# Strided convolution with normalisation, forward and backward: first weights over a second hardware queue, two elementwise stages of the second batch on ScalarE, and a re-planned order

## The chip, the core and the metric

The kernel runs on one core of a Trainium2 chip. The core has TensorE (PE: matmuls, with its weight loads shown as PEld), VectorE (DVE), ScalarE (ACT), GpSimd (POOL) and SyncE (SP). DMAs are issued by SP, ACT and POOL, each into a queue of its own; the packets of all three run on the same 16 DMA engines. Each engine works through its own instructions in the order of the program and waits on semaphores for the others. The metric is the device time of one execution in microseconds. Before the change it was 1239.66 us, the median of three runs from 1238.98 to 1240.63.

## The reference

Everything is bfloat16 at the interface: `x` (2, 16000, 256), `w` (31, 256, 256), `gn_gamma` and `gn_beta` (256).

```
L = (16000 - 31) // 2 + 1 = 7985
h[b,l,:]  = sum_i x[b, 2*l + i, :] @ w[i]            i = 0..30
mu, var   = mean and variance of h over l, per b and channel
hn        = (h - mu) / sqrt(var + 1e-5) * gamma + beta
out_0     = gelu(hn)                                  (tanh form)
out_1..4  = gradients of x, w, gamma, beta for the given grad_out (2, 7985, 256)
```

So there are three large products: the forward convolution, its input gradient and its weight gradient. Between the first and the second lies the elementwise part (normalisation, gelu, its derivative, and sums over l).

## The kernel before

**Stages.** The plan names five. F0 is the forward convolution of batch 0 and F1 that of batch 1; under F1 the gelu part of batch 0 runs on ACT and DVE. G0 is the input gradient of batch 0, with the gelu part of batch 1 under it. G1 is the input gradient of batch 1, with the differences that the weight gradient needs (`d2_piece`) under it. W is the weight gradient. A batch is cut into four chunks `c`; a chunk has three branches `br` (B_, A, C_), and in the gradient two halves `pr`. The products are built from sums and differences of inputs and of weights, three in place of four, and that at three levels, so each branch starts with a product (`f_three_b`, `g_three_b`), lets ACT copy it negated within PSUM (L540, L1060), goes on with `three_ac` products, is combined by DVE in PSUM (`f_seed`, `g_seed`, which record `ve` at L583), and ends in `leaf` products whose result ACT moves out (`f_evac`, `g_evac`: L611 or `keep` at L591). PSUM is a ring of four tiles; a branch takes two.

**The start.** `x_load` (L399) brings the odd rows of the first chunk as three plain loads (two of 512 KB, one of 64 KB). PE turns them by matmuls (`x_first`, L419), DVE and ACT put them into SBUF (L431, L429). `load_w` (L443) brings the weights: 16 loads, slots A and C_, two channel halves `ch`, all on SP's queue behind x. `f_first` (L706) forms weight differences on DVE (`w_sub`, L466) and starts the first leaf products. All later chunks of x come as one transposing DMA on SP's queue (`turn`, L346).

**The gelu part.** `gelu_unit` (L829) works on 1024 columns: a load of h on ACT's queue (the `hd` tensor), four ACT instructions (L836, L838, L842, L844), several DVE ones, a store on POOL's queue, a sum on ACT (L860).

**Between gelu and input gradient.** For each chunk `e_load` (L928) loads dy and h (1 MB each) on SP's queue, and `e_comp` (L932) computes h*s5 + s6 (L938), dy*s4 (L941) and their sum (L943) on 2048 columns twice, then spreads the result into padded tiles (four copies: two of 1536 columns, two of 512). The spread goes by `COPY = ("ACT", "DVE")`: on ACT (L953) for batch 0, on DVE (L955) for batch 1. `dn_turn` (L977) transposes the same result and stores it.

**What sets the order.** No operation is emitted where it is written. `Plan.add` records each with its engine, an assumed duration, what it reads and writes, and for a DMA its transfer time. `Plan.order` gives each a due time from the PE work that needs it (less a `slack`, and less a `lead` that is set by hand for each kind of operation), and plays a list schedule: at each engine the ready operation that is due first goes next. PE may take any of the next `look` operations of its own list. `pads` hold a DMA back behind what it depends on; DMAs share one server that takes them one after another, and eight lanes per queue group. The operations are then emitted in the order of their planned starts, and the engines keep that order. `PACE` spreads the gelu units over the PE work. Planned times are used for nothing else.

Of the kernel before, what the change touches and what calls it, by code (L numbers as in the profile page):

```python
# [13 lines left out]
ALU = mybir.AluOpType  # L14
# [24 lines left out]
class Plan:  # L39
# [3 lines left out]
    def __init__(self, tc):  # L43
        self.tc = tc
        self.ops = []
        self.lastw = {}
        self.readers = {}
        self.pe = 0.0
        self.slack = 120.0
        self.hold = -1  # L50
        self.look = 11
        self.pads = (270.0, 253.5, 0.0)
        self.lead = {
            "F0 f_mm f_leaf": 4.0,
            "F0 f_mm f_outer": -1.5,
            "F0 f_mm f_three_ac": 5.5,
            "F0 f_mm pe_turn": 7.5,
            "F0 f_three_b forward": -7.5,
            "F0 keep f_evac": -4.0,
            "F0 load f_evac": 10.5,  # L60
            "F0 load load_w": -2.5,
            "F0 load put": 2.0,
            "F0 tt f_sums": 7.5,
            "F0 tt third": -5.0,
            "F0 turn w2_part": -1.5,
            "F0 turn x_load": -5.0,
            "F0 ve f_seed": -2.0,
            "F0 w_sub f_first": 7.5,
            "F1 f_evac last": -7.5,
            "F1 f_mm f_leaf": -5.0,  # L70
            "F1 f_mm f_three_ac": 1.5,
            "F1 gelu_unit gelu_batch": -3.0,
            "F1 load gelu_unit": 2.5,
            "F1 tiny fwd_stats": -4.0,
            "F1 tt gelu_unit": 1.0,
            "F1 turn gelu_batch": -6.5,
            "F1 turn x_load": -5.0,
            "F1 ve f_seed": 6.5,
            "F1 zero gelu_batch": 11.0,
            "G0 e_comp conv_stem_kernel": -3.0,  # L80
            "G0 g_mm g_leaf": -11.0,
            "G0 g_mm g_three_ac": 5.0,
            "G0 g_mm g_three_b": -4.0,
            "G0 gelu_unit gelu_batch": -0.5,
            "G0 keep g_evac": -3.5,
            "G0 load dgb_store": 7.0,
            "G0 load dn_turn": -8.0,
            "G0 load e_load": 4.5,
            "G0 load g_evac": -8.0,
            "G0 load gelu_unit": 10.0,  # L90
            "G0 load load_w2": 5.0,
            "G0 tiny elem_finalize": 1.5,
            "G0 tt first": 5.0,
            "G0 tt second": 6.0,
            "G0 tt third": 5.5,
            "G0 turn dgb_store": -3.0,
            "G0 turn dn_turn": 1.0,
            "G0 turn gelu_batch": -8.5,
            "G0 ve g_seed": 3.5,
            "G0 ve_neg g_seed": 8.0,  # L100
            "G1 e_comp conv_stem_kernel": -10.0,
            "G1 g_mm g_outer": 3.5,
            "G1 g_mm g_three_ac": 0.5,
            "G1 g_mm g_three_b": 0.5,
            "G1 g_three_b input_grad": 2.5,
            "G1 keep g_evac": -3.5,
            "G1 load dn_turn": 0.5,
            "G1 load e_load": -4.0,
            "G1 load g_evac": 5.5,
            "G1 spread e_comp": -9.5,  # L110
            "G1 tt first": 10.5,
            "G1 tt second": -4.5,
            "G1 tt third": -5.0,
            "G1 zero e_comp": -5.0,
            "W keep weight_grad": 4.0,
            "W load d_tile": -15.5,
            "W load w_emit": -8.5,
            "W ve w_done": 5.0,
            "W ve weight_grad": 9.0,
            "W w_add weight_grad": 2.5,  # L120
            "W w_emit w_done": 7.5,
            "W w_mm w_pairs": -1.5,
            "W w_mm w_single": -1.0,
        }
        self.overlap = {"DVE": 0.084, "ACT": 0.1}
        self.npe = 0
        self.stage = "F0"
# [23 lines left out]
    def add(self, eng, dur, outs, ins, fn, dma=None, slack=None):  # L151
# [24 lines left out]
        self.ops.append(dict(eng=eng, kind=kind, dur=dur, fn=fn, preds=preds, dma=dma, at=self.pe, hold=-1 if eng == "PE" else self.hold,  # L176
# [3 lines left out]
    def order(self):  # L180
# [7 lines left out]
        for i in range(n - 1, -1, -1):  # L188
            o = ops[i]
            full = o["dur"] + (1.3 * o["dma"] + 6.0 if o["dma"] is not None else 0.15)  # L190
            end = o["at"] if o["eng"] == "PE" else o["at"] + o["slack"]
            for s in succ[i]:
                end = min(end, due[s])
            due[i] = end - full - self.lead.get(o["kind"], 0.0)
        left = [len(o["preds"]) for o in ops]
        ready = [0.0] * n
        wait = {e: [] for e in ("PE", "DVE", "ACT", "POOL", "SP")}
        pes = [i for i, o in enumerate(ops) if o["eng"] == "PE"]
        rank = {i: k for k, i in enumerate(pes)}
        nextpe = 0  # L200
        gone = set()
        lanes = [[0.0] * 8, [0.0] * 8]
        for i in range(n):
            if not left[i]:
                wait[ops[i]["eng"]].append(i)
        free = {e: 0.0 for e in wait}
        server = 0.0
        start = [0.0] * n
        ends = [0.0] * n
        done = 0  # L210
        while done < n:
            best = None
            for e, w in wait.items():
                if e == "PE":
# [3 lines left out]
                if w:  # L218
                    t = max(free[e], min(ready[i] for i in w))
                    if best is None or t < best[0]:  # L220
                        best = (t, e, w)
            t, e, w = best
            i = min((i for i in w if ready[i] <= t + 1e-9), key=lambda i: (due[i], i))
            wait[e].remove(i)
            o = ops[i]
            if o["dma"] is not None:
                lane = lanes[e == "POOL"]
                t = max(t, lane.pop(0))
            start[i] = t
            end = t + o["dur"]  # L230
            free[e] = end - self.overlap.get(e, 0.0)
# [5 lines left out]
            if o["dma"] is not None:  # L237
                server = max(server, end + 1.3) + o["dma"]
                end = server + 0.9
                lane.append(end)  # L240
            ends[i] = end
            done += 1
            slip = free["PE"] - due[pes[nextpe]] - ops[pes[nextpe]]["dur"] if nextpe < len(pes) else 0.0
            for s in succ[i]:
                r = end + 0.034 * (e != "PE") if ops[s]["eng"] == e and o["dma"] is None else end + 0.12
                room = max(0.0, due[s] + slip - r)
                if ops[s]["dma"] is not None:
                    r += min(self.pads[0 if o["dma"] is None else 1], 0.3 * room)
                elif o["dma"] is not None and ops[s]["eng"] != "PE":
                    r += min(self.pads[2], 0.3 * room)  # L250
                ready[s] = max(ready[s], r)
                left[s] -= 1
                if not left[s]:
                    wait[ops[s]["eng"]].append(s)
        self.start, self.ends = start, ends
        return sorted(range(n), key=lambda i: (start[i], i))
# [13 lines left out]
def conv_stem_kernel(  # L270
# [64 lines left out]
    def dcost(nbytes, run):  # L335
        ns = {256: 18, 512: 27, 1024: 46, 2048: 85, 4096: 165}[run]
        return nbytes / run * ns / 16e3 * 1.1
# [1233 lines left out]
```

## Time and profile before

| What | us |
|---|---|
| median of three runs | 1239.66 (1238.98 to 1240.63) |
| the profiled execution | 1234.47 |
| its span, first to last instruction | 1232.3 |
| PE busy in the span | 1195.2 (97%) |
| DVE busy | 1010.3 (82%) |
| ACT busy | 535.8 (43%) |
| POOL busy | 203.7 (17%) |
| mean granted TensorE clock | 0.992 |
| DMA | 263.56 MB, mean 214 GB/s |

The profiled execution is 5.2 us shorter than the median of the runs; its span covers all but 2.2 us of it. PE is busy nearly throughout, so what counts is where PE waits and for whom. The profile gives for each wait its length and the instruction that ended it last; a matmul that runs at a lower granted clock is busy, not waiting, so after a long wait the clock column has to be read as well.

### The profile page before, as it was taken

How to read it: one execution, taken by the hardware profiler on the slowest of the kernel's cores; microseconds unless marked ns; L12 is line 12 of the kernel's file. 1: busy time of each engine (PE TensorE's matmuls, PEld its weight loads, DVE VectorE, ACT ScalarE, POOL GpSimd, SP SyncE). 2: the span in 40 equal slices, each digit the busy share in tenths (PEclk: the TensorE clock that was granted, in tenths of full speed). 3: DMA queues.
4: the chain of work that ended last, by engine and by line, in shares of the span. 5: the costliest groups of instructions: out<-in, count | busy, mean ns of one | idle time of the engine just before them, and what ended most of it. 6: DMA issues, size and time to landing. Idle time of an engine off the chain costs nothing.

```text
span 1232.3 us, 19408 instructions
## 1 busy us (share of the span) xinstructions
PE 1195.2 (97%) x7846; PEld 768.7 (62%) x7846; DVE 1010.3 (82%) x1297; ACT 535.8 (43%) x769; POOL 203.7 (17%) x321
## 2 busy tenths in 40 slices
PE   6999999899999999999999999999999999999998
PEld 4888899577676964444444444444466554566865
DVE  7988798597979859989887889888776986778883
ACT  1243344565768468888783334444322111012200
POOL 1020231011111203211210323333210000011031
PEclk8999999899999999999999999999999999999999
DMA  9642979866695896686636888886899499986562
GB/s 205 108 111 63 191 198 177 168 139 158 127 201 159 258 317 208 231 248 168 213 120 182 254 273 313 245 308 251 300 305 326 145 318 319 320 293 218 179 170 69
DMA packets 283545, 263.56 MB, mean 214 GB/s; under 512 B 186815, under 2 KB 254446, under 8 KB 275184
## 3 DMA queue, kind: packets, MB, share of 16 engines
q1 hardware_dynamic: 255808, 166.38, 52.5%
q0 software_dynamic: 23040, 87.55, 20.1%
q10 hardware_dynamic: 4608, 8.39, 2.3%
q8 instruction: 61, 1.00, 0.3%
q14 instruction: 28, 0.23, 0.1%
HBM read 129.44 MB, written 87.52 MB: 176 GB/s over the span
## 4 chain that ended last, share of the span: by engine, by line
PE 79%; DVE 6%; DMA 6%; issue 4%; ACT 2%; POOL 2%; SPq 0%; POOLq 0%; ACTq 0%; DVEq 0%
PE ps L508 31%; PE ps L1289 27%; PE ps L1033 21%; DMA d2d<-arena 2%; DMA arena<-hd 1%; DVE arena L1196 1%; POOL d2d L341 1%; DVE arena L476 1%; DMA out_dram<-arena 1%; DVE ps L583 1%; DMA arena<-in_x_dram 1%; DVE arena L466 1%; DMA arena<-arena 1%; DMA arena<-in_w_dram 1%; DVE arena L943 0%
## 5 line engine op out<-in xcount | busy, mean ns | idle before, releaser
L1033 PE MATMUL ps<-arena 128*128 128x512 bf16 (+1 forms) x2016 | 435.9, 378 | 11.8 <-DVE ps L583 8.3
L508 PE MATMUL ps<-arena 128*128 128x256 bf16 (+4 forms) x3552 | 426.7, 282 | 12.6 <-DMA arena<-in_x_dram 6.9
L508 PEld LDWEIGHTS <-arena 128*128 128x128 bf16 x3552 | 347.8, 99 | 94.4 <-issue 13.7
L1033 PEld LDWEIGHTS <-arena 128*128 128x128 bf16 x2016 | 198.0, 98 | 249.4 <-issue 20.1
L1289 PE MATMUL ps<-arena 128*128 128x256 bf16 (+1 forms) x2176 | 332.5, 313 | 0.0
L1289 PEld LDWEIGHTS <-arena 128*128 128x128 bf16 x2176 | 212.8, 98 | 112.6
L591 ACT ACTIVATE arena<-ps 128x1024 f32<-128x1024 f32 (+1 forms) x143 | 146.1, 1022 | 277.8 <-PE ps L1033 79.9
L476 DVE TENSOR_TENSOR arena<-arena 128x1087 bf16<-128x1087 bf16 (+3 forms) x194 | 163.7, 889 | 27.5 <-PE ps L508 27.2
L850 DVE TENSOR_TENSOR arena<-arena 128x1024 bf16<-128x1024 bf16 x160 | 109.0, 689 | 14.8 <-ACT arena L842 8.2
L1252 DVE TENSOR_TENSOR arena<-arena 128x4096 bf16<-128x4096 bf16 x42 | 95.8, 2288 | 25.2 <-PE ps L1289 19.6
L583 DVE TENSOR_TENSOR ps<-ps,arena 128x1024 f32<-128x1024 f32 x77 | 94.0, 1229 | 27.0 <-PE ps L1289 13.3
L341 POOL DMA_DIRECT2D out_dram<-arena x75 | 54.1, 741 | 365.7 <-DVE arena L1321 292.0
L992 DVE TENSOR_TENSOR arena<-arena 128x516 bf16<-128x516 bf16 (+3 forms) x176 | 83.5, 513 | 16.4 <-PE ps L1033 10.0
L1196 DVE TENSOR_TENSOR arena<-arena 128x768 bf16<-128x768 bf16 (+3 forms) x112 | 65.5, 642 | 16.7 <-DMA d2d<-arena 15.6
L341 POOL DMA_DIRECT2D d2d<-arena x70 | 51.0, 729 | 112.3 <-DVE arena L1196 110.7
L611 ACT ACTIVATE arena<-ps 128x512 bf16<-128x512 f32 (+1 forms) x64 | 36.8, 578 | 74.5 <-PE ps L508 74.5
L840 DVE SCALAR_TENSOR_TENSOR arena<-arena 128x1024 bf16<-128x1024 bf16 x32 | 39.2, 1224 | 20.1 <-ACT arena L838 19.8
L583 DVE TENSOR_TENSOR ps<-arena,ps 128x1024 f32<-128x1024 f32 x43 | 52.8, 1227 | 3.2 <-PE ps L1033 2.7
L1370 ACT COPY ps<-ps 128x512 f32<-128x512 f32 x28 | 16.0, 571 | 87.6 <-PE ps L1289 87.6
L1060 ACT ACTIVATE ps<-ps 128x512 f32<-128x512 f32 x48 | 27.9, 582 | 58.8 <-PE ps L1033 58.6
L1413 DVE TENSOR_TENSOR arena<-arena 128x2304 bf16<-128x2304 bf16 x36 | 48.0, 1354 | 5.5 <-PE ps L1289 5.5
L341 POOL DMA_DIRECT2D dyd<-arena x32 | 17.6, 550 | 194.2 <-DVE arena L850 189.5
(87 smaller groups left out, 785.8 us busy)
## 6 DMA issues: line engine op xcount, KB each, us to landing
arena<-in_x_dram SPq DMA_DIRECT2D x52, 1024.0 KB, 9.6
arena<-d2d SPq DMA_DIRECT2D x16, 1216.0 KB, 11.9
out_dram<-arena POOLq DMA_DIRECT2D x14, 1024.0 KB, 5.9
d2d<-arena POOLq DMA_DIRECT2D x30, 384.0 KB, 6.3
arena<-dnd SPq DMA_DIRECT2D x10, 960.0 KB, 6.4
vl<-arena POOLq DMA_DIRECT2D x36, 256.0 KB, 4.8
arena<-vl SPq DMA_DIRECT2D x9, 1024.0 KB, 8.6
hd<-arena POOLq DMA_DIRECT2D x8, 1024.0 KB, 6.3
```

The lines of the kernel that those rows point to most:

```text
L341: add(eng, issue or {"POOL": 0.8, "SP": 0.4, "ACT": 0.15}[eng], [out], [in_], lambda: e.dma_start(out=out, in_=in_), dma=dcost(nbytes, run ...
L476: lambda: nc.vector.tensor_tensor(out=o, in0=a, in1=b, op=ALU.add))
L508: yield nc.tensor.matmul(ps[:, dh, cs], lhsT=wt, rhs=mv, start=s0, stop=False, skip_group_check=True)
L583: add("DVE", dve(1024, 1), [out], [a, b], lambda: nc.vector.tensor_tensor(out=out, in0=a, in1=b, op=op))
L591: lambda: nc.scalar.activation(out=out, in_=ps, func=ACT.Copy, scale=scale))
L850: add("DVE", dve(1024), [o], [a, b_], lambda: V.tensor_tensor(out=o, in0=a, in1=b_, op=op))
L992: lambda: nc.vector.tensor_tensor(out=o, in0=a, in1=b, op=ALU.add))
L1033: yield nc.tensor.matmul(ps[:, e, 0:wide], lhsT=lt, rhs=mv, start=s0, stop=False, skip_group_check=True)
L1196: lambda: nc.vector.tensor_tensor(out=out, in0=a, in1=b_, op=ALU.subtract))
L1252: add("DVE", dve(4096), [o], [a, b], lambda: nc.vector.tensor_tensor(out=o, in0=a, in1=b, op=ALU.add))
L1289: yield nc.tensor.matmul(ps[:, s, c0:c1], lhsT=lt, rhs=mv, start=s0, stop=False, skip_group_check=True)
L1413: add("DVE", dve(2304), [DL[i3, b]], [D2[b]], lambda b=b, i3=i3, o_=o_: nc.vector.tensor_tensor(out=DL[i3, b], in0=D2[b][:, o_:o_ + 17:2, ...
```

## The change

Four things change.

- The 64 KB load of x and the four weight loads of slot A, `ch` 0, are issued on ACT's queue; the other loads of x and of the weights stay on SP's. The 64 KB load is recorded first.
- `e_comp` of batch 1 does both affine steps on ACT (activations with scale and bias taken from tiles) in place of DVE, and its spread on ACT too.
- The planner's picture of DMAs is replaced. `listing` lets three queues move packets at the same time: on each queue the oldest transfer is active, and active transfers share the engines by the packet time of their shape (`tp`), with a factor `mixed` where transposes run beside others. SP's queue blocks while more than `room` packets are on their way. The costs of an issue and of packets (`SH`, `PK`) are new.
- The hand-set numbers follow: `slack`, `look`, `pads`, all of `lead`, `PACE`. Every engine's order over the whole kernel is therefore new. The set of operations is the same but for the queue and engine moves above: 7846 matmuls in both.

```diff
-        self.slack = 120.0
+        self.slack = 110.0
-        self.look = 11
-        self.pads = (270.0, 253.5, 0.0)
+        self.look = 13
+        self.pads = (375.5, 347.0, 2.5)
         self.lead = {
-            "F0 f_mm f_leaf": 4.0,
...
+            "F0 f_mm f_leaf": 12.5,
...
         }
+        self.room, self.mixed = 2048.0, 1.4
...
+        def flow(t):
+            nonlocal now
+            if total > 0:
+                for x in air:
+                    if x["act"]:
+                        x["rem"] -= (t - now) * x["tp"] / total
+            now = t
+
+        def inflight():
+            return sum(x["rem"] * 16e3 / ops[x["i"]]["ns"] for x in air if ops[x["i"]]["eng"] == "SP")
...
+            heads = {}
+            for x in air:
+                x["act"] = heads.setdefault(ops[x["i"]]["eng"], x) is x and x["on"]
+            total = sum(x["tp"] for x in air if x["act"])
+            if total > max((x["tp"] for x in air if x["act"]), default=0.0) and any(ops[x["i"]]["ns"] < 20.0 for x in air if x["act"]):
+                total *= self.mixed
...
             if o["dma"] is not None:
-                server = max(server, end + 1.3) + o["dma"]
-                end = server + 0.9
-                lane.append(end)
+                k = e == "POOL"
+                air.append(dict(i=i, on=False, act=False, lane=turn[k], rem=o["dma"], tp=o["tp"], t0=end + 1.3))
+                lanes[k][turn[k]] = 1
+                turn[k] = (turn[k] + 1) % 8
+                if e == "SP" and inflight() > self.room:
+                    blocked, spend = True, end
+                continue
...
-            for g, nm in enumerate((P, P, 16)):
-                load(rows[g][0:nm], src[P * g:P * g + nm].rearrange("m (j o f) -> m j o f", j=4, o=2)[:, :, 1, :], nm * 4096, 1024)
+            for g, nm in ((2, 16), (0, P), (1, P)):
+                load(rows[g][0:nm], src[P * g:P * g + nm].rearrange("m (j o f) -> m j o f", j=4, o=2)[:, :, 1, :], nm * 4096, 1024,
+                     "ACT" if g == 2 else "SP")
...
-                         65536 * nq, 512, issue=0.8)
+                         65536 * nq, 512, "ACT" if sl == A and ch == 0 else "SP")
...
-    COPY = ("ACT", "DVE")
+    COPY = ("ACT", "ACT")
...
+            if b == 0:
+                add("DVE", dve(2048, 4), [hv], [hv, s5, s6], ...
+                add("DVE", dve(2048, 4), [ev], [ev, s4], ...
+            else:
+                add("ACT", act(2048, 0.18), [hv], [hv, s5, s6],
+                    lambda hv=hv, s5=s5, s6=s6: nc.scalar.activation(out=hv, in_=hv, func=ACT.Identity, bias=s6, scale=s5))
+                add("ACT", act(2048, 0.18), [ev], [ev, s4],
+                    lambda ev=ev, s4=s4: nc.scalar.activation(out=ev, in_=ev, func=ACT.Identity, scale=s4))
...
-    PACE = ((5.0, 19.0), (391.0, 67.0))
+    PACE = ((20.0, 16.5), (327.0, 54.0))
```

What the new order does at the places the prediction speaks of, read from the two programs (line numbers of the kernel before):

- Start: the weights of both slots for `ch` 0 are loaded before those for `ch` 1, and the leaf products run in that order (A and C_ with `ch` 0, then with `ch` 1); before, slot A came first with both halves.
- Start of F1: on ACT the first load of h, then the square root of the statistics, then the `keep` (L591) of batch 1's first result stand ahead of the first gelu unit; before, two loads of h came first and that `keep` stood behind five instructions of two gelu units. The second load of h now stands behind that `keep`. The big transposing load of x (chunk 1) stays near the same place on SP's queue.
- Chunk 2 of F1: `f_three_b`'s two halves are separated by a leaf product.
- Start of G0: the first `g_three_b` stands ahead of the last two leaf groups of F1 on PE, and its ACT copy ahead of the last evacuations.
- End of G1: the addition of two x tiles for the weight gradient (`w_add`, L1252) that stood between two of the last `g_seed` instructions on DVE stands behind them.

271 lines of the change are left out of this document (155 added, 116 removed).

## The prediction

> **What bounds the kernel now.** I read the busy shares first, then who ends PE's waits, then the places of those waits in order of time.
>
> ```profile
> PE 1195.2 (97%) x7846; PEld 768.7 (62%) x7846; DVE 1010.3 (82%) x1297; ACT 535.8 (43%) x769; POOL 203.7 (17%) x321
> ...
> PE ps L1033 <- DVE ps L583: 8.3, 9, 2.4
> PE ps L508 <- DMA arena<-in_x_dram: 6.9, 2, 4.6
> PE ps L508 <- ACT arena L591: 6.1, 1, 6.1
> PE ps L508 <- DVE arena L476: 4.0, 1, 4.0
> PE ps L508 <- ACT arena L611: 3.5, 2, 1.9
> PE ps L1033 <- ACT arena L611: 2.1, 1, 2.1
> PE ps L1033 <- ACT ps L1060: 0.8, 1, 0.8
> PE ps L1033 <- ACT arena L591: 0.6, 2, 0.3
> ```
>
> PE works 97% of the span, and no matmul is added or removed, so only PE's waits can move the time: 32.3 us in all, 10.9 of them (x, and L476) in the first 15 us, 21.4 later. A wait also lowers the granted clock: 0.95 over 240 to 300 us, 0.94 over 450 to 480, 0.97 over 850 to 900, which is 60*0.05 + 30*0.06 + 50*0.03 = 6.3 us of missing clock. What the new order can win after the start is thus at most 27.7 us. W has no wait of PE from 895 to 1224 us: nothing to win there.
>
> The largest wait, in order of time:
>
> ```profile
> 216.92 20.43 SPq L346 DMA_TRANSPOSE arena<-in_x_dram  x1
> ...
> 219.53 0.91 ACTq L341 DMA_DIRECT2D arena<-hd  x2
> ...
> 232.73 1.24 ACT L836 ACTIVATE arena<-arena,stats 128x1024 bf16<-128x1024 bf16 x1 [10.14 <-DMA arena<-hd]
> ...
> 240.37 1.01 ACT L591 ACTIVATE arena<-ps 128x1024 f32<-128x1024 f32 x1
> ...
> 241.42 0.37 PE L508 MATMUL ps<-zt 128*128 128x256 bf16 x1 [6.11 <-ACT arena L591]
> ```
>
> Two loads of h (256 KB each) are issued 2.6 us into a 20.43 us transposing load of x; ACT stands still for 10.14 us until they land; the `keep` at L591 is queued behind, and PE waits for it. Other loads of this kind take 4.6 us (median): here the queues collide on the shared engines.
>
> The input gradient of batch 1, and the operations that move:
>
> ```profile
> 680.00:720.00 40.00, 37.92 (x179) 17.31 (x178) 33.16 (x48) 16.04 (x22) 11.82 (x18) 1.00 0.89 276
> 720.00:760.00 40.00, 38.82 (x180) 17.35 (x179) 38.68 (x62) 16.23 (x23) 13.52 (x19) 1.00 0.86 275
> ...
> L938 DVE TENSOR_SCALAR arena<-arena,stats 128x2048 bf16<-128x2048 bf16 x16 | 12.6, 812 | 3.5 <-DMA arena<-hd 3.5
> L941 DVE TENSOR_SCALAR arena<-arena,stats 128x2048 bf16<-128x2048 bf16 x16 | 11.7, 750 | 0.0
> L955 DVE COPY arena<-arena 128x1536 bf16<-128x1536 bf16 x8 | 4.2, 559 | 0.0
> L953 ACT COPY arena<-arena 128x1536 bf16<-128x1536 bf16 x8 | 11.6, 1464 | 2.9 <-issue 2.7
> ```
>
> DVE (third column of busy time) is full here, ACT (fourth) at 40%, and all waits of PE but 0.6 us are ended by DVE's `g_seed` (L583).
>
> **The change part by part.** Gains are negative; the bounds stand behind each.
>
> *Start.* SP issued 16 weight loads one after another, 2.81 to 18.41 us; DVE's first `w_sub` waited for one until 12.66, and the first leaf product began at 15.14. Five DMAs leave SP for ACT. Their issue costs 0.33 us each (hd rows): 1.7 us, plus the table load 1.28, before an ACT whose first copy was needed at 9.86; the fifth waits until the 64 KB load has landed (5.5 us), which still ends before. POOL is not touched. x (512 KB twice, landed 7.2) now shares the engines with 1 MB of weights. 2048 packets of 512 B took 3.6 us, 1024 of 1 KB 3.0; taken in turn, x lands about 1.8 us later, the first weights about 1 us earlier. x is then last: PE's turning (3.92 us from 7.19), two copies, `w_sub` 1.23 and the sum 1.29 start the leaf products near 14.5. Gain 0.6; bounds +2 (all of x's delay passes on) and -2 (the 2.3 us wait for x goes). The busy time by stretches shows DMA at 1.11 of the 16 engines from 10 to 20 us, so the engines, not the issue, limit the end of these loads; therefore a value near nothing. The Trainium skill, "DMA: Bandwidth & Descriptors", section "Rules for kernel authors", says that spreading DMAs over SP, ACT and GpSimd gives no bandwidth and saves issue time alone. The 1.11 agrees; by that rule the term would be 0 and the sum 0.6 higher.
>
> *F1's start.* The 241 us place costs 6.1 of wait and 2.0 of slow clock (18 matmuls in 1.91 + 2.67 us where eight take 1.04 at full clock). The `keep` now stands ahead of the gelu units, so this wait goes. What is late next: the second load of h is still issued into the same transposing load, and ACT's next `f_three_b` copy (L540) stands behind its reader. It landed at 235.6, two readers take 2.4, so the copy is done near 239; PE, running on from 235.1, has 2 us of first products and 6 us of leaf work ahead of it. If the load is 3 us later still, 2.6 us are lost. I take -5.5 (0 to -8.1).
>
> *319 and 390 us.* Waits of 1.92 and 1.60 for evacuations (L611) queued behind gelu instructions; at the first, 4.2 us of them. In the new order a leaf product covers the first; the second I cannot tell: -2.5 (0 to -3.5).
>
> *G0's start.* Waits of 2.12, 0.80 and 0.64 from 450 to 481 and 1.8 of clock. Two leaf groups (28 matmuls of 230 columns each, 2.8 us by the 118 that took 11.87 us from 435.77) now lie between the first `g_three_b` and the product that needs its copy; the evacuations on ACT are covered. -3.5 (0 to -5.4).
>
> *G1, DVE.* Batch 1 takes from DVE 8*0.812 + 8*0.750 + 8*0.559 + 8*0.298 (the 512 copies) = 19.4 us. PE's waits there before the last are 8.3 - 0.64 - 2.40 + 0.6 = 5.9 us. About half goes, since `d2_piece` also waits for its stores (15.6 us of DVE's idle time): -3 (0 to -5.9).
>
> *G1, ACT.* No row has an activation over 2048 columns. From 1024 columns with two tile operands (L838, 1.234) and the slope of L953 ((1.464 - 0.614)/1024 columns) it takes 1.234 + 0.85 = 2.08 us. 16 of these, 8 copies of 1.464 and 8 of 0.614 add 49.9 us. ACT from 620 to 895 goes from 41-44% to about 60%. From 500 to 600 us ACT was busy 85.0 of 100 us with instructions of 0.6 to 1.5 us, and PE did not wait once; so a busy ACT is hidden by PE's leaf work as long as nothing ACT waits for is late. The cost is taken as +2, near that row (0 to +18, below).
>
> *890 us.* The last `g_seed` stood behind `w_add`, which waited for x until 886.4: wait 2.40, clock 1.5. `w_add` moves behind; the weight gradient's first product then needs x, 2.3 + 1.2 us of DVE later, and PE has some 5 us before it. -3 (0 to -3.9).
>
> *New waits.* Every engine's order is new, so there will be waits that the old order did not have. The old one had 27.7 us of such cost; I allow about a fifth, +5 (0 to +27.7).
>
> Sum: -0.6 - 5.5 - 2.5 - 3.5 - 3 + 2 - 3 + 5 = -11.1. From the profiled execution, 1234.5 - 11.1 = 1223.4; the median of the runs lay 5.2 above the profiled one, so 1228.6, rounded to 1229.
>
> **The rivals.**
> *ACT blocks the second batch (slower).* For chunks 1 to 3 `e_comp` on ACT waits for two 1 MB loads, with `keep` and copies queued behind. At 232 us such a wait of 10.14 us gave PE one of 6.11, 0.6 of it. Three times 10.14 would cost 18.3 us instead of +2 and take the 3 us of DVE with it: 1229 + 19 = 1248. It decides from about 7 us per chunk (three times 0.6*7 = 12.6, against 11.1 + 2). For it: DMA at 0.85 in this stretch, these loads take 6.4 and 8.5 us. Against: before, DVE waited for them once, 3.5 us. The Trainium skill, "ScalarE: Activation LUTs", "Rules for kernel authors", advises VectorE for multiply and add, being up to about three times faster in bf16. The rows agree (0.81 against the estimate of 2.08), and the advice speaks for this rival.
> *Contention stays (same).* The h load lands as late and blocks ACT at the next copy, DVE's relief is eaten by stores: 5.5 + 3 less gain, 1237.5, between 1235 and 1242.
> *Hidden better (faster still).* No new waits, all of DVE's share: 1229 - 5 - 3 = 1221.
> *W begins to wait (slower).* DMA is at 0.83 to 0.95 from 900 to 1100 and 9.6 us is the median of an x load; three late pairs of 5 us: 1244.
>
> **How the numbers follow.** Forecast 0.45, ACT blocks 0.2, contention stays 0.15, hidden better 0.12, W waits 0.08. 0.2% of the time, 2.5 us, is about what can be told from no change, so same is 1237.2 to 1242.1. Faster: 0.45*0.95 + 0.12 + 0.15*0.4 + some of the last = 0.64; same 0.11, mostly contention; slower 0.25 from ACT and W. The likeliest case alone lies in 1223 to 1236. The range reaches from 1218 (everything hidden) to 1247 (ACT blocks by nearly its full price) and leaves out about 0.2.
>
> **What will show it.** Right: no wait of PE near 241 us ended by L591's counterpart; the first leaf product near 14.5; the waits on `g_seed` in G1 down by about half; activations of 2048 columns at 2.0 to 2.1 us; W still without waits. Wrong: waits of PE ended by ACT in G1 above 5 us in sum, ACT waiting for hd or dyd there, or new waits in F0, where PE did not wait between 15 and 235 us.

## The result and the profile after

The changed kernel takes 1250.59 us (median of 20 runs, 1239.76 to 1256.90), the kernel before 1237.56 (median of 20; 19 of them from 1230.80 to 1245.38, and one of 4483.74, which the median passes over). The ratio is 1.0105, 95% interval 1.0079 to 1.0130: 13 us slower, where 1229 (1218 to 1247) was predicted. The profiled execution took 1246.25 us, its span 1244.5.

Where PE waits now, longest first (the view of waits: us in total, times, longest):

```profile
PE ps L575 <- DMA arena<-in_x_dram: 9.2, 2, 5.1
PE ps L1106 <- DVE ps L650: 8.5, 11, 2.9
PE ps L1362 <- DMA arena<-d2d: 7.7, 2, 4.0
PE ps L575 <- ACT ps L607: 6.4, 2, 5.7
PE ps L575 <- DVE arena L543: 4.5, 1, 4.5
```

Three of these lines are new or longer: the start waits more for x (9.2 against 6.9), the wait of 6.1 for the `keep` at F1's start has become one of 5.7 for a copy (L607), and W, which had no wait, waits 7.7 for d. Against the waits on `g_seed` (L650) little was won: 8.5 in 11 waits, 8.3 in 9 before.

To see what each stage lost or won, I took from each trace the times at which PE's 1750th, 3598th, 4600th, 5614th and last of its 7846 weight loads start. They cut the span near the ends of F0, F1, G0, G1 and W; the orders differ by a few groups of matmuls at the cuts.

| span of (us) | F0 | F1 | G0 | G1 | W | rest | whole |
|---|---|---|---|---|---|---|---|
| before | 207.0 | 240.4 | 218.7 | 228.7 | 332.4 | 5.1 | 1232.3 |
| after | 210.6 | 242.1 | 215.7 | 227.6 | 343.3 | 5.1 | 1244.5 |
| after less before | +3.6 | +1.7 | -3.0 | -1.1 | +10.9 | 0 | +12.2 |

So in this pair of profiles the loss lies in W above all, and in the start. The place in W, on SP's queue and on PE:

```profile
895.38 8.74 SPq L412 DMA_TRANSPOSE arena<-yd  x1
904.31 4.42 SPq L407 DMA_DIRECT2D arena<-in_x_dram  x2
908.82 22.48 SPq L412 DMA_TRANSPOSE arena<-yd  x1
931.40 1.00 SPq L407 DMA_DIRECT2D arena<-d2d  x2
...
937.47 0.60 PE L1362 MATMUL ps<-arena 128*128 128x256 bf16 x4 [4.00 <-DMA arena<-d2d]
941.81 1.01 PE L1362 MATMUL ps<-arena 128*128 128x256 bf16 x4 [3.74 <-DMA arena<-d2d]
```

and SP's queue in the kernel before:

```profile
888.14 17.57 SPq L346 DMA_TRANSPOSE arena<-yd  x2
905.83 1.28 SPq L341 DMA_DIRECT2D arena<-in_x_dram  x2
907.19 3.43 SPq L341 DMA_DIRECT2D arena<-d2d  x2
```

The second column is the time SP was held. `yd` holds y, the gelu output of batch 1 that is transposed late on its way to out_0; `d2d` holds d, the differences that the weight gradient reads. A transposing load of y (1 MB) that took 8.74 us a moment earlier holds SP for 22.48; the two loads of d stand behind it, are issued at 931.4 and come late. In the kernel before both loads of y came one right after the other, and d was issued at 907.19.

F1's start, the same view on SP, ACT and PE:

```profile
223.51 23.57 SPq L412 DMA_TRANSPOSE arena<-in_x_dram  x1
...
243.15 1.24 ACT L903 ACTIVATE arena<-arena,stats 128x1024 bf16<-128x1024 bf16 x1 [13.60 <-DMA arena<-hd]
...
252.97 0.58 ACT L607 ACTIVATE ps<-ps 128x512 f32<-128x512 f32 x1
...
253.60 9.75 PE L575 MATMUL ps<-arena 128*128 128x256 bf16 x56 [5.70 <-ACT ps L607]
```

The wait at 241 us is gone as the `keep` now runs at 228.5, but its cause is as it was: x's transposing load takes 23.57 us (20.43 before), ACT stands still 13.60 us (10.14) for the first load of h, and the copy at L607, behind two gelu units, is the next that PE misses. The size varies: in five other profiles with this order of F1 (the runs d_first, head_on_sp, late_y_plain, affine_on_dve and no_out_store below) the wait here is 4.6, 9.4, 11.1, 11.9 and 15.9 us.

The start, on PE and DVE, after and then before:

```profile
9.52 3.49 PE L575 MATMUL ps<-arena 128*128 128x128 bf16 x31 [4.10 <-DMA arena<-in_x_dram]
...
18.51 7.69 PE L575 MATMUL ps<-arena 128*128 128x512 bf16 x35 [4.50 <-DVE arena L543]
...
15.50 1.22 DVE L533 TENSOR_TENSOR arena<-arena 128x2048 bf16<-128x2048 bf16 x1 [2.08 <-DMA arena<-in_w_dram]
```

```profile
15.14 11.14 PE L508 MATMUL ps<-arena 128*128 128x512 bf16 x55 [4.03 <-DVE arena L476]
12.66 1.23 DVE L466 TENSOR_TENSOR arena<-arena 128x2048 bf16<-128x2048 bf16 x1 [0.25 <-DMA arena<-in_w_dram]
```

x is complete at 9.5 us (7.2 before), and the weights of the first `w_sub` (L533) at 15.5 (12.7). The leaf products begin at 18.51 instead of 15.14. The DMA view of 9 to 13 us (queue: packets, MB, share of 16 engines), after and then before, shows why the weights are later:

```profile
q10 hardware_dynamic: 1209, 0.60, 57.5%
q1 hardware_dynamic: 1133, 0.56, 54.5%
```

```profile
q1 hardware_dynamic: 2317, 1.15, 116.3%
```

The engines move as much as before, 1.16 MB in 4 us. But the four loads that this `w_sub` needs are ScalarE's (q10), and half of what moves is SP's (q1): weights that nobody needs yet. On one queue the needed ones came first.

The input gradient of batch 1 (busy time by stretches), and what ScalarE took over:

```profile
680.00:720.00 40.00, 38.47 (x176) 17.41 (x178) 33.69 (x49) 25.59 (x28) 13.00 (x20) 1.00 0.95 274
720.00:760.00 40.00, 36.24 (x168) 16.39 (x170) 34.17 (x52) 27.29 (x30) 12.96 (x21) 1.00 0.98 289
...
L1012 ACT ACTIVATE arena<-arena,stats 128x2048 bf16<-128x2048 bf16 x8 | 16.4, 2090 | 0.0
L1014 ACT ACTIVATE arena<-arena,stats 128x2048 bf16<-128x2048 bf16 x8 | 15.6, 2000 | 5.0 <-DMA arena<-dyd 5.0
```

ACT is busy 53 of 80 us here (32 before), and DVE 68 (72 before); PE is a little busier in the first stretch (37.92 before) and less in the second (38.82).

### The profile page after: what moved, and what is told of

Its sections match the earlier page's. It is cut to its first block, busy times and chain, and to the rows that moved or that the text cites. A ratio compares the mean times of both kernels' runs of the same rounds, so it can differ in the third digit from the quotient of the medians.

```text
span 1244.5 us, 19368 instructions
## 1 busy us (share of the span) xinstructions
PE 1191.3 (96%) x7781; PEld 768.8 (62%) x7846; DVE 994.6 (80%) x1265; ACT 579.3 (47%) x801; POOL 200.8 (16%) x321
## 4 chain that ended last, share of the span: by engine, by line
PE 62%; DVE 10%; issue 10%; DMA 9%; ACT 5%; POOL 3%; SPq 0%; POOLq 0%; DVEq 0%; ACTq 0%
PE ps L575 25%; PE ps L1362 24%; PE ps L1106 13%; DMA arena<-hd 3%; DVE arena L917 3%; DMA d2d<-arena 2%; POOL d2d L407 2%; DMA out_dram<-arena 1%; DVE ps L650 1%; DVE arena L1269 1%; DVE arena L907 1%; DMA arena<-in_w_dram 1%; DMA arena<-d2d 1%; ACT arena L678 1%; DVE arena L543 1%
## 5 line engine op out<-in xcount | busy, mean ns | idle before, releaser
L1106 PE MATMUL ps<-arena 128*128 128x512 bf16 (+1 forms) x1974 | 430.2, 376 | 15.5 <-DVE ps L650 8.5
L1106 PEld LDWEIGHTS <-arena 128*128 128x128 bf16 x2016 | 197.0, 98 | 248.2 <-issue 12.7
L1362 PEld LDWEIGHTS <-arena 128*128 128x128 bf16 x2176 | 213.5, 98 | 122.4 <-issue 9.4
L543 DVE TENSOR_TENSOR arena<-arena 128x1088 bf16<-128x1088 bf16 (+3 forms) x194 | 162.9, 887 | 13.4 <-PE ps L575 12.9
L917 DVE TENSOR_TENSOR arena<-arena 128x1024 bf16<-128x1024 bf16 x160 | 108.5, 689 | 23.8 <-ACT arena L909 15.5
L650 DVE TENSOR_TENSOR ps<-ps,arena 128x1024 f32<-128x1024 f32 x77 | 93.6, 1227 | 19.8 <-PE ps L1362 14.4
L1065 DVE TENSOR_TENSOR arena<-arena 128x514 bf16<-128x514 bf16 (+3 forms) x176 | 81.1, 511 | 7.2 <-PE ps L1106 4.4
L650 DVE TENSOR_TENSOR ps<-arena,ps 128x1024 f32<-128x1024 f32 x43 | 52.7, 1226 | 12.0 <-PE ps L1106 8.7
L678 ACT ACTIVATE arena<-ps 128x512 bf16<-128x512 f32 (+1 forms) x64 | 36.9, 580 | 52.3 <-PE ps L575 52.1
L650 DVE TENSOR_TENSOR arena<-arena 128x1024 f32<-128x1024 f32 x32 | 38.4, 1221 | 28.0 <-ACT arena L640 17.2
L1486 DVE TENSOR_TENSOR arena<-arena 128x2304 bf16<-128x2304 bf16 x36 | 48.2, 1353 | 12.7 <-PE ps L1362 12.7
L407 POOL DMA_DIRECT2D vl<-arena x36 | 26.1, 726 | 158.5 <-DMA arena<-in_w_dram 99.8
## 6 DMA issues: line engine op xcount, KB each, us to landing
arena<-d2d SPq DMA_DIRECT2D x16, 1216.0 KB, 10.9
```

The costliest lines, as they stand in the source:

```text
L407: lambda: e.dma_start(out=out, in_=in_), dma=np_ * PK[pk] / 16e3 * 1.03, ns=PK[pk], tp=SH[pk], slack=slack)
L543: lambda: nc.vector.tensor_tensor(out=o, in0=a, in1=b, op=ALU.add))
L650: add("DVE", dve(1024, 1), [out], [a, b], lambda: nc.vector.tensor_tensor(out=out, in0=a, in1=b, op=op))
L917: add("DVE", dve(1024), [o], [a, b_], lambda: V.tensor_tensor(out=o, in0=a, in1=b_, op=op))
L1065: lambda: nc.vector.tensor_tensor(out=o, in0=a, in1=b, op=ALU.add))
L1106: yield nc.tensor.matmul(ps[:, e, 0:wide], lhsT=lt, rhs=mv, start=s0, stop=False, skip_group_check=True)
```

## The experiments

All were compared with the kernel before on the same chip. A line of the table gives the ratio with its interval and the stage spans of the profile, cut as above; what each run changes is told below. The spans are of one execution each. F1 moves most by itself: it is 241.7 to 251.9 us in the six profiles that have the changed kernel's order and transfers there (the changed kernel, head_on_sp, late_y_plain, d_first, no_out_store, affine_on_dve). W is 343.3 to 346.8 in the six that have them there.

| run | ratio | F0 | F1 | G0 | G1 | W |
|---|---|---|---|---|---|---|
| head_on_sp | 1.0103 (1.0069-1.0137) | 207.9 | 245.8 | 216.6 | 227.3 | 345.9 |
| late_y_plain | 1.0035 (1.0007-1.0062) | 208.3 | 247.5 | 215.1 | 228.4 | 332.4 |
| d_first | 1.0001 (0.9967-1.0034) | 209.7 | 241.7 | 215.6 | 227.3 | 333.6 |
| no_out_store | 0.9989 (0.9948-1.0031) | 209.2 | 251.9 | 215.1 | 227.4 | 332.4 |
| f1_x_plain | 1.0033 (1.0008-1.0058) | 210.7 | 233.4 | 215.1 | 230.4 | 346.3 |
| no_h_store | 1.0026 (0.9986-1.0066) | 210.4 | 242.9 | 215.1 | 226.8 | 346.8 |
| tiny_h_loads | 0.9983 (0.9955-1.0010) | 210.1 | 233.0 | 215.1 | 229.5 | 346.0 |
| h_first | 0.9967 (0.9946-0.9988) | 210.3 | 236.4 | 215.9 | 228.1 | 333.6 |
| all_three | 0.9971 (0.9949-0.9993) | 208.0 | 236.9 | 215.1 | 228.5 | 333.6 |
| all_three_dve | 1.0032 (1.0010-1.0054) | 208.2 | 235.6 | 215.1 | 238.2 | 333.6 |
| affine_on_dve | 1.0128 (1.0086-1.0170) | 209.1 | 247.9 | 215.1 | 233.7 | 344.4 |
| planner_only | 1.0131 (1.0084-1.0178) | 207.4 | 238.6 | 215.5 | 237.3 | 340.0 |
| before_queue | 1.0017 (0.9989-1.0046) | 213.5 | 242.5 | 220.1 | 225.5 | 332.6 |
| before_act | 1.0181 (1.0143-1.0219) | 209.8 | 239.1 | 221.6 | 225.6 | 352.8 |
| before_h | 0.9953 (0.9932-0.9973) | 209.6 | 234.8 | 221.4 | 224.1 | 337.8 |
| before_h_act | 1.0034 (1.0010-1.0058) | 208.1 | 233.1 | 223.3 | 233.3 | 333.9 |

### W: is it the order on SP?

First, the late loads of y as plain loads, at the same places:

```
-        turn(o.rearrange("p r a d -> p (r a) d"), y_d[c][:], 1 << 20)
+        turn(o.rearrange("p r a d -> p (r a d)"), y_d[c].rearrange("(p q) f -> p (q f)", q=2), 1 << 20, plain=True)
```

> The changed kernel, same order, with the four late loads of y in the weight gradient made as plain loads of the same megabyte instead of transposing ones (those rows of out_0 are then not transposed). Theory (the loads of d behind a transposing load of 22.5 us on SP are what PE waits for at 937 and 942 us): the two waits of 4.0 and 3.7 us and the slow clock behind them go, 9 to 10 us less, ratio about 1.003. Rival (the shared engines are full there and d would be late in any case): waits of 5 us or more stay at this place, ratio 1.007 or more.

W fell to 332.4 us, the span it had before the change, and no wait for d is left. On SP's queue d is issued 17 us earlier than in the changed kernel, in a run that is 3 us later by the end of G1:

```profile
907.99 4.01 SPq L407 DMA_DIRECT2D arena<-in_x_dram  x2
912.09 1.98 SPq L412 DMA_DIRECT2D arena<-yd  x1
914.17 4.16 SPq L407 DMA_DIRECT2D arena<-d2d  x2
```

As many bytes move, but two things differ: SP isn't held, and the packets are larger (SP's queue moved 11.86 MB in 7845 packets from 903 to 946 us, 7.44 MB in 10363 in the changed kernel). Then with y transposed as it should be, by one entry in the planner's table, which puts d ahead:

```
+            "W turn out0_late": -25.0,
```

> The changed kernel with one lead added to the planner's table that puts the two loads of d for the weight gradient's second branch ahead of the two transposing loads of y on SP; up to there the order is the same. Theory (order on SP, not the amount of data, makes d late): no wait of PE for d near 940 us, the weight gradient takes 332 to 335 us from its first product to its last instead of 343 to 346, ratio about 1.002. Rival (the engines are full, what is put behind is late in turn): waits of PE for x or for products of DVE of 5 us or more in its place, ratio 1.006 or more.

```profile
907.93 1.42 SPq L407 DMA_DIRECT2D arena<-d2d  x1
909.40 13.51 SPq L412 DMA_TRANSPOSE arena<-yd  x1
```

The loads of y still transpose, and d no longer stands behind them. The ratio is 1.0001 (0.9967 to 1.0034) and W 333.6, with no wait for d: one entry gives back the loss. Then what makes the load of y so long:

```
-            load(dst, o[0:r, :, a, :], r * 4096, 512, "POOL", slack=60.0)
+            cut = (lambda dst=dst, r=r, a=a: nc.gpsimd.dma_start(out=dst[:, 0:1, :], in_=o[0:r, 0:1, a, :])) if c < 2 else None
+            load(dst, o[0:r, :, a, :], r * 4096, 512, "POOL", slack=60.0, fn=cut)
...  (the last store of out_1 likewise)
```

> The changed kernel, same order, with GpSimd's last store of out_1 and its two late stores of each of the first two chunks of out_0 cut to small pieces (most of those rows are not written). Theory (GpSimd's stores stretch the transposing loads of y): the second load of y takes at most 12 us instead of 19 to 22.5, d's loads are issued by 920 us, the waits for d fall below 3 us, ratio about 1.003. Rival (x's loads ahead of it in the queue stretch it): it still takes 17 us or more and the waits stay, ratio 1.009 or more.

```profile
911.79 4.01 SPq L407 DMA_DIRECT2D arena<-in_x_dram  x2
915.89 10.38 SPq L412 DMA_TRANSPOSE arena<-yd  x1
926.37 1.01 SPq L407 DMA_DIRECT2D arena<-d2d  x2
```

The loads of x are still ahead, the load of y takes 10.38 us instead of 22.48 (22.4 to 25.6 in the five other profiles with this order of W), and no wait for d is left (d is issued at 926.4, not by 920, in a run that is 7.5 us later by the end of G1). So in W it is GpSimd's stores, in the third queue, that hold up the transposing load, and SP's order that hands this on to d.

### F1's start

x's transposing load as a plain one of as many bytes:

```
+            if (b, c) == (1, 1):
+                turn(flat[:, :, 0:nr], bass.AP(tensor=x.tensor, offset=x.offset + b * T * C, ap=[[32 * nr, P], [nr, 32], [1, nr]]),
+                     nr * 8192, plain=True)
+            else:
                 turn(flat[:, :, 0:nr], src, nr * 8192)
```

> The changed kernel, same order, with the one load of x that is issued at 223.5 us made as a plain load of as many bytes instead of a transposing one (x of the second chunk of batch 1 is then wrong). Theory (this transposing load holds up the two loads of h on the second queue, and with them ScalarE and the copy PE waits for): the wait of 5.7 us at 253.6 and the slow clock behind it go, about 8 us less, ratio about 1.004; loads of h land within 6 us. Rival (any transfer of 2.2 MB there would do the same): the wait stays above 4 us, ratio 1.009 or more.

As the theory had it, but for 0.2 us on h: F1 233.4, the wait at this place gone (0.4 in all on the copy), h lands after 6.2 us (median; 16.9 in the changed kernel), x itself after 10.0 (28.5). What stretches the transposing load was then tried from both sides. Without GpSimd's store of h:

```
+                    if (b, c) == (0, 3):
+                        yield nc.gpsimd.dma_start(out=h_d[0][3][:, 0:256], in_=hf[:, 0:256])
```

> The changed kernel, same order, with the store of h of batch 0's last chunk (1 MB, issued by GpSimd at 225 us) cut to 64 KB; the rest of that chunk of h is a copy of the chunk before, stored 40 us earlier. Theory (GpSimd's store is what stretches the transposing load of x from 10 to 24 us): x's load takes at most 12 us, h's loads land within 8, the wait of PE near 253 us falls below 2, ratio about 1.004. Rival (the loads of h beside it stretch it): x's load still takes 18 us or more, the wait stays at 5 to 12 us, ratio 1.009 or more.

and without the loads of h:

```
+        cut = (lambda: nc.scalar.dma_start(out=hf[:, 0:64], in_=hv[:, 0:64])) if (b, c) == (0, 0) and 2 * e + dh < 3 else None
```

> The changed kernel, same order, with the first three loads of h of the gelu pass (256 KB each, issued by ScalarE beside x's transposing load) cut to 16 KB. Theory (it is the traffic in GpSimd's queue, h's store and the weight stores before it, that stretches x's load): x's load still takes 18 us or more. Rival (the loads of h stretch it): it takes 12 us or less. The wait near 253 us goes in either case, since the small loads land early, or stays where even they are held up; ratio about 1.004.

x's load held SP 19.98 us without the store and 18.16 with the small loads of h. That is less than in any of the six profiles with the transfers whole, 23.2 to 34.0 us, and more than twice the 8.31 us that it takes alone (below): each of the two alone leaves a large part. Without the store the waits here were 2.6 and 2.8 us and the ratio was near the theory's, but the load's time is the rival's, so neither is borne out as a whole; F1 (242.9) is no shorter than in the changed kernel's profile, where the wait was 5.7. With the small loads F1 fell to 233.0, the ratio to 0.9983 (1.004 was expected) and the wait to 0.3 in all, though x's load stayed long as the theory had it: the first load of h landed after 5.5 us, and the first gelu unit ran early. The other two, of 16 KB like it, still took 11.4 and 10.2 us to land, so it isn't their own size that makes them late. GpSimd's queue still carries 256 KB weight stores in both runs. Beside such traffic the transposing packets nearly stop, as the DMA view (queue: packets, MB, share of 16 engines) of 230 to 240 us of the changed kernel shows, with q1 SP's, q0 GpSimd's and q10 ACT's queue:

```profile
q1 hardware_dynamic: 1085, 0.28, 46.4%
q0 software_dynamic: 279, 1.45, 46.0%
q10 hardware_dynamic: 270, 0.49, 20.9%
```

and with the queues to itself, in the run h_first from 232 to 240 us:

```profile
q1 hardware_dynamic: 8244, 2.10, 122.8%
```

SP's queue moved 0.28 MB in 10 us against 2.10 in 8. How the delay divides between the store, the weight stores and h at this place stays open.

The remedy is again an order. The first three loads of h go on SP's queue, ahead of x:

```
-        load(h.rearrange("p k f -> p (k f)"), hv, 262144, 2048, "ACT")
+        if (b, c) == (0, 0) and 2 * e + dh < 3:
+            load(h.rearrange("p k f -> p (k f)"), hv, 262144, 2048, slack=0.0)
+        else:
+            load(h.rearrange("p k f -> p (k f)"), hv, 262144, 2048, "ACT")
```

> The kernel of the run d_first, in which also the first three loads of h for the gelu pass are issued by SP ahead of the transposing load of x at 220 us, instead of by ScalarE beside it. Theory (at F1's start it is again the order of transfers, not their amount, that makes h late): no load of h takes over 6 us there, ScalarE does not stand still for one, the copy's wait near 255 us (6 to 12 us in the runs so far) goes, ratio about 0.993. Rival (x is late in its place): a wait of 5 us or more on the next chunk's sums near 260 us, ratio 0.999 or more.

```profile
222.79 2.36 SPq L407 DMA_DIRECT2D arena<-hd  x3
225.20 6.55 SPq L412 DMA_TRANSPOSE arena<-in_grad_out_dram  x1
231.86 8.31 SPq L412 DMA_TRANSPOSE arena<-in_x_dram  x1
```

x starts 8 us later than in the changed kernel and SP is through with it 7 us earlier. The copy's wait is gone, F1 is 5 us shorter than in d_first, and the ratio is 0.9967: faster than the kernel before. It is less than the 0.993 expected: h took 7.9 us to land instead of 6, and waits for evacuations (L680, L678 in the runs without the edit) rose from 2.4 us in d_first to 5.3. The same edit alone in the old kernel:

> The kernel before with nothing changed but the first three loads of h, issued by SP ahead of the transposing load of x at 217 us instead of by ScalarE beside it (old planner; the order on the engines moves only within F1). Theory (the wait at F1's start is one of the old kernel too, has nothing to do with the new order, and goes with the order on SP): no wait on a keep or copy of ACT near 241 us, ratio 0.993 to 0.996. Rival (the old order of ScalarE holds the keep up in any case, or x is late in its place): ratio 0.998 or more.

0.9953, the lowest ratio of all (its interval overlaps those of h_first and all_three): 1228.69 us beside 1235.72. So this loss belongs to the old kernel as much as to the new, and three load instructions win what the new order was to win here. (A wait of 3.6 us for d in W shows in its profile.)

### The start

> The changed kernel with x's small piece and the four first weight loads issued by SP again, in the old order; the planned order differs only within the first chunks. Theory (splitting the first loads over two queues makes x and the first weights land later, because both queues draw on the same 16 engines): the first leaf product goes back from 18.5 to about 15.1 us and the time falls by 3 us, ratio to the kernel before about 1.008. Rival (the late start is made up later by shorter waits of F0): first leaf product at 15.1, but the same time, 1.0105.

The edit is the inverse of the two parts of the diff that move the first loads. The leaf products began at 15.05 us, and F0 ended 2.7 us earlier, so nothing of it is made up within F0. In the time it doesn't show: F1 and W of this profile were longer by 3.7 and 2.6 us, and the interval is wider than the effect, so the runs leave the theory and its rival open.

The queue alone, put into the old kernel:

> The kernel before with the five first loads issued by ScalarE and nothing else changed (old planner; its order moves only in the first chunks). Theory (the second queue delays the start): first leaf product at 17 to 18.5 us instead of 15.1, ratio 1.002 to 1.003. Rival (the start is late only because the new order puts a weight difference ahead of the fifth copy and the sum on VectorE): first leaf product at 15 to 16 us, ratio 1.000.

The start got later than either theory said: the leaf products began at 22.60 us. PE's turning of x stopped for 5.87 us, since DVE's copies of it (L432) stand behind a `w_sub` that waited until 15.26 for its weights. In the changed kernel only the last, small copy stands behind it. F0 is 6.5 us longer; the ratio of 1.0017 doesn't exclude 1. Last, all three remedies together:

> The kernel of the run h_first with the five first loads on SP as in the kernel before. Theory (the second queue at the start costs 2 to 3 us): first leaf product at 15.1 us, ratio about 0.991, below that of h_first by 0.002. Rival (made up later): the ratio of h_first.

0.9971, not below h_first. The leaf products began at 16.2 (17.9 in h_first), F0 is 2.3 us shorter in the profile, and the runs do not show it.

All profiles together tell more than a pair. The leaf products begin at 15.05 to 16.93 us (mean 15.9) in the eight with the five loads on SP, and at 17.00 to 18.51 (mean 18.0) in the changed kernel and the eight runs that keep its start. So the queue costs about 2 us there; in the times it isn't told from nothing. It is not x that comes late by it: x is complete at 7.1 to 9.2 us without the second queue and at 7.1 to 9.5 with it. It is the weights: the first `w_sub` waits 2.0 to 3.6 us for them in each of the nine, and at most 0.55 in the eight.

### ScalarE's share

Every instruction at its place in the list, but on VectorE again:

```
-                    lambda hv=hv, s5=s5, s6=s6: nc.scalar.activation(out=hv, in_=hv, func=ACT.Identity, bias=s6, scale=s5))
+                    lambda hv=hv, s5=s5, s6=s6: nc.vector.tensor_scalar(out=hv, in0=hv, scalar1=s5, scalar2=s6,
+                                                                        op0=ALU.mult, op1=ALU.add))
...  (the second pass and the copies likewise)
```

> The changed kernel, every instruction at its place in the planned list, but the second batch's affine pass and spread run on VectorE again. Theory (the move to ScalarE gave a little in G1, since VectorE's g_seed is what PE waits for there): waits of PE on L650 in G1 rise from 6.5 to about 9 us, the time by 2 to 4 us, ratio 1.013. Rival (ScalarE's load in G1 costs more than it gives): the time falls by 2 us or more, ratio 1.009 or less.

> The kernel of the run all_three, every instruction at its place in the planned list, but the second batch's affine pass and spread on VectorE again. Theory (the move to ScalarE gives 3 to 5 us in G1, also where nothing else waits): ratio about 0.003 above that of all_three, 1.000, waits of PE on products of DVE (the counterpart of L650) in G1 12 us or more against 8.8. Rival (it gave only because the order was planned for it and F1 was late): the ratio of all_three, 0.997.

The first is muddied by F1 and W: its ratio is the theory's, but the changed kernel's own lies within its interval, and only G1 (233.7 against 227.6) and the waits on L650 (13.1 in all against 8.5) show the move. The second is clear: 1.0032 against 0.9971, 0.6% or 7.5 us, with G1 238.2 against 228.5 and the other stages within 1.3 us. PE's waits on `g_seed`, in all_three and then in all_three_dve:

```profile
PE ps L1111 <- DVE ps L652: 8.8, 10, 2.3
```

```profile
PE ps L1112 <- DVE ps L652: 14.3, 10, 3.0
```

In the old kernel the move lost time. Planned anew:

> The kernel before with the second batch's affine pass and spread on ScalarE and nothing else changed (old planner and table, planned again). Theory (the move gives 3 to 5 us in G1): ratio 0.996 to 0.998. Rival (ScalarE's loaded queue holds up keep and the copies that PE waits for): ratio 1.003 or more, with waits of PE ended by ACT in G1 above 5 us.

G1 is 3.1 us shorter, as the theory had it, and PE's waits ended by ACT in G1 are 2.4 us, so the rival's reason isn't there. But W is 20 us longer: planned again, SP's order there became y, x, y, x, d, and PE waits 12.0 us for d. With the list of before_h kept:

> The kernel of the run before_h with its planned list kept as it is, but the second batch's affine pass and spread on ScalarE. Theory (the 1.8% of the run before_act came from the new order of SP in the weight gradient, not from ScalarE's load): the waits of PE in the weight gradient are those of before_h, G1 is 3 to 5 us shorter, ratio 0.991 to 0.994. Rival (in the old order, which has no room for it on ScalarE, the 50 us of added work hold up keep and copies): G1 5 us or more longer, ratio 0.999 or more.

W is free of that (333.9), as the theory had it, but G1 is 9.2 us longer than in before_h, and the time 0.8% more. PE's waits for ACT in G (L591 with its copy L1063 or L1064), before_h and then before_h_act:

```profile
PE ps L1036 <- ACT ps L1063: 2.2, 3, 0.8
...
PE ps L1036 <- ACT arena L591: 1.9, 3, 1.4
```

```profile
PE ps L1037 <- ACT arena L591: 7.6, 8, 2.5
...
PE ps L1037 <- ACT ps L1064: 3.3, 2, 2.5
```

For G1 in this order the theory is refuted and the rival holds. ACT waits for no load of h or dy in G1 here; what is left as the cause is its own added work, at places planned for VectorE; no run takes that apart further. And the new planner without either move:

> The changed kernel without both moves of work: the first loads on SP, affine pass and spread on VectorE, but the new model of the queues and its table. Theory (the new order costs the time, in F1 and in the weight gradient): F1's wait near 250 us and the wait for d near 940 us are both there, ratio 1.009 to 1.013. Rival (the late start and ScalarE's load cost the time): ratio 1.003 or less.

1.0131: the slowdown is the planner's. W waits 5.6 us for d, and G1 takes 237.3, 8.6 us more than in the old order with the same work on DVE; F1's wait was small in this profile (2.5). So in G1 the new order loses about 9 us, and the move to ScalarE wins them back: that is why G1 stood at -1.1. PE's waits on `g_seed` are 13.4 us in all here against 8.3 before; what in the new order makes them stays open.

## Why the prediction was wrong

By the profiles the sum was -11.1 and came out at +12.2, a miss of 23.3 us. Of it 10.9 lie in W, 9.7 in F1 (-8.0 forecast for its places together, +1.7 measured), 4.2 in the start, 2.9 in G1 and 0.5 in G0, less the 5 that was allowed for new waits.

*W.* The step that failed first is the one that put W at nothing in the sum: "W has no wait of PE from 895 to 1224 us: nothing to win there". It was true of the old order, and it left out that a new order can lose there. W was among the rivals only as late pairs of x (0.08); what came was d, late by its place behind a transposing load: +10.9 us, the largest part of the miss and nearly the whole measured loss. Under "new waits" +5 stood for all of them, with an upper end of 27.7; W alone took twice the 5, and the place wasn't looked for. It could have been: the order on SP in W was to be read from the program, and the profile of before has a stretched load (20.43 us at 217 us, shown in the prediction) beside one of the same tensor that takes 9.79 at 269 us.

*F1's start.* Predicted -5.5 (0 to -8.1). The collision was named ("the second load of h is still issued into the same transposing load, and ACT's next copy stands behind its reader"), but the step failed that took the second load alone as late, with two readers (2.4 us) between it and the copy. The first load came late too: issued at 224.83, it landed at 243.0, and the second at 245.6, not near 238.6. So both gelu units, 9.8 us on ACT, stood between h and the copy, which ran at 252.97, not near 242. The wait moved by 12 us and stayed; the bound of 0 was too kind, as other profiles of this order show up to 15.9. This was the rival "contention stays".

*Start.* Predicted -0.6 (bounds -2 to +2), measured +3.4 at the first leaf product in this pair of profiles, and about +2 between the means of all. The step "the first weights about 1 us earlier" failed: they came 2.8 us later (15.50 against 12.66), for the needed ones share the engines with SP's, which were behind them before. For x 1.8 us of delay were predicted; x came 2.3 us later here, but it varies as much without the second queue, so that agreement is luck. The Trainium skill, "DMA: Bandwidth & Descriptors", section "Rules for kernel authors", says that spreading gives no bandwidth and saves issue time alone; the trace agrees on the bandwidth (1.16 and 1.15 MB in 4 us), but shows a price.

*319 and 390 us, G0's start.* -2.5 and -3.5 predicted. PE's idle time from 300 to 420 us fell by 1.6, from 3.52 to 1.96 us, and G0 by 3.0: both within their bounds, the second about right.

*G1.* DVE's relief (-3), ACT's cost (+2) and the place at 890 us (-3, no wait of PE is left there) sum to -4; measured -1.1. The sum hides two larger numbers that the prediction didn't have: the new order itself costs some 9 us here, and the move gives 6 to 10, so that the total came within 3 us of the forecast is luck. The prediction called DVE full here; by its own rows that holds for the second stretch (38.68 of 40 us) and less for the first (33.16). The activations took 2.00 and 2.09 us, as worked out from the slope (2.08). The rival "ACT blocks the second batch" did not come to pass in the new order: ACT waited for dyd 1.83 and 3.13 us there and PE's waits on ACT in all of G are 2.9 us. In the old list ACT did hold PE up (before_h_act), but not by waiting for loads, as the rival had it. The Trainium skill's advice for VectorE ("ScalarE: Activation LUTs", "Rules for kernel authors") agrees with the rows, 0.81 against 2.09 us, and yet the slower engine was the better place once the order had room for it.

*The signs.* Two of those named came: no wait near 241 us, and the activations as priced. Three did not: the leaf products near 14.5, the halved waits on `g_seed`, W without waits. Of the signs of wrong one was seen, small: ACT waited for dyd in G1, 5.0 us in all. The largest loss lay where no sign of wrong had been set.

## What to carry over

A list of instructions planned anew can fail wherever the old one was free of waits, so a stage without waits is not safe: read the new order on the queues there, too. Look in the profile of before for transfers whose time varies at equal size, and in the new order for what stands behind them on the same queue. The two largest steps here came from that: three loads put ahead of a transposing one gave 0.5% in the old kernel, with nothing else of the change, and one entry for d gave back the 1% that the new order had lost.

## What was not expected of the hardware

In these traces a transposing load was as fast as its company let it be. The same 2176 KB of x held SP 8.31 us alone and 18 to 34 us beside GpSimd's stores and other loads (18.16 in tiny_h_loads, 23.57 in the changed kernel, 34.04 in no_out_store), while a plain load of as many bytes at that place held it 0.35 us and landed in 10.0. The Trainium skill, "Advanced Engine Details and Errata", section "X-Bar Transpose (TRN2)", says that such transfers are as fast as regular ones; that comes near the load alone (11.9 us to landing in h_first, beside 10.0 for the plain one), and differs from the load in company (28.5 against 10.0).
